# Attention running up to 1.9 batches ahead of the FFN, stores without one-row DMAs, and sparser filler matmuls

## The chip, the core and the metric
The kernel runs on one core of a Trainium2 chip. The metric is the device time of one execution in microseconds (us). The program is one launch; its instruction streams are fixed when it is built, one per engine: TensorE (PE), VectorE (DVE), ScalarE (ACT), GpSimd (POOL) and SyncE (SP). Engines wait for one another by semaphores only, and each works through its own stream in order.

## What is computed
Two stages, for 8 batches, 12 heads, 448 rows, head size 64 (model size 768), first layer of the FFN 3072 wide:

```
scores = (q @ k.T) / 8
x      = (relu(scores) ** 2 / 448) @ v          # heads side by side: 448 x 768 a batch
u      = x + real(fft(fft(x, axis=rows), axis=columns))
un     = (u - mean(u)) / sqrt(var(u) + 1e-6)    # over the 768 columns
out    = u + relu(un @ w_ch1) @ w_ch2
```

q, k, v, both weights and the output are float32 in HBM; matmuls are in bf16.

## The kernel before
**Attention** of a batch is 24 steps of two heads and one of four row chunks. A step is two scores matmuls into a psS buffer (L441), a relu on ACT into rsc (L473), a square on DVE into sq (L467), and two values matmuls into psT (L455). Four steps make one 128-column piece m of x, transposed (xT). DVE folds row s with row 448 - s into sums and differences (`fold`, L389 to L398), so that the Fourier transforms become real matmuls over 225 rows, and an SP DMA transposes xT back to rows (xn, L407). q and k are first copied (qkr, L339) and transposed, in batch 0 on TensorE, later by SP DMAs (qkT, L347). The loads of q, k, v and of the weights (w) are issued on POOL in one order; a q or k load waits for its buffer's copy, a v load for the values matmuls that read its buffer.

**Mix** of a batch: 24 matmuls (L618) with the column matrices `chan`, copies to pc (ACT L629, DVE L631), then in two chunks of rows, SC = 0 to 127 and 128 to 224, the row matmuls (L502), their evacuation (qs on ACT, tm and tp on DVE), the sums u for the upper rows (DVE) and mirrored lower rows (POOL; DVE in batch 0), the statistics (L535, L536), std on ACT (L539), and un on ACT (L549). u and un go to DRAM scratch: the upper rows by plain SP DMAs (utop, ntop), the lower ones, which come out in reverse order, by an indirect DMA on POOL (ubot, nbot, L569). The second chunk of the lower half has 97 rows, whose row 96 is row 0 of ubot and nbot: a one-row SP DMA writes it (L567), ahead of the indirect DMA of the other 96.

**FFN** works on groups of rows: 384 and 512 in turn, since group 2i takes the first 384 rows of batch 2i and group 2i+1 its last 64 with all of batch 2i+1. The transposed rows unT come from ntop and nbot by SP DMA transposes (`turn_un`, L592); only in group 0 TensorE transposes un (L651) and ACT copies it (L654). 24 blocks of six matmuls (L712) each with a relu into hT (L702) make the first layer; the second is 24 matmuls (L747) for each 128 rows and half of the columns, added to u (o, L729) and stored. psF has two buffers, psS and psT two each.

**The order** of all this is made when the program is built, by a planner (`Streams.run`): every part is a generator that announces its next piece of work with an engine, a cost in us, due times and buffers, and the planner always emits the piece that can start first by its own clock. Attention's pieces come last as long as `progress`, the FFN's share done in batches, is below `lead`:

```
lead = b + p / NP - LEAD
e = yield need("PE", dur + SWITCH, deps, bufs, lambda: progress[0] >= lead)
```

`warming` fills TensorE with 128x256 matmuls on zeros (L765) until the FFN begins. It too is planned: a filler is put wherever the planner believes TensorE to be idle, and on the chip it runs in its place, whether TensorE is idle then or not. `build_dft` makes the Fourier matrices from angles: products on DVE (L234, L243), reduction to one turn on DVE (L218, L220), sine on ACT (L222).

Of the kernel before, what the change touches and what calls it, by code (L numbers as in the profile page):

```python
# [9 lines left out]
FP32 = mybir.dt.float32  # L10
BF16 = mybir.dt.bfloat16
AF = mybir.ActivationFunctionType
ALU = mybir.AluOpType

# [28 lines left out]
class Streams:  # L43
    def __init__(self):
        self.engine = dict.fromkeys(LATENCY, 0.0)
        self.streams = []
        self.dma_free = 0.0
# [4 lines left out]
    def dma(self, start, nbytes, rate=350e3):  # L52
        self.dma_free = max(self.dma_free, start + 1.0) + nbytes / rate
        return self.dma_free + 1.2
# [60 lines left out]
def kernel(  # L115
# [9 lines left out]
    nc = tc.nc  # L125
# [12 lines left out]
    SC = [(0, 128), (128, NS)]  # L138
# [10 lines left out]
    ubot = [dram.tile([HS + 1, D], FP32, name=f"ubot{b}") for b in range(B)]  # L149
    ntop = [dram.tile([HS, D], BF16, name=f"ntop{b}") for b in range(B)]  # L150
    nbot = [dram.tile([HS + 1, D], BF16, name=f"nbot{b}") for b in range(B)]
# [17 lines left out]
    eps_t = const.tile([128, 1], FP32, name="eps_t")  # L169
    ident = const.tile([128, 128], BF16, name="ident")  # L170
# [11 lines left out]
    def dft_indices():  # L182
        nc.gpsimd.iota(drow[:, 0:2], pattern=[[128, 2]], base=0, channel_multiplier=1,
                       allow_small_or_imprecise_dtypes=True)
        nc.gpsimd.iota(drow[:, 4:7], pattern=[[128, 3]], base=0, channel_multiplier=1,
                       allow_small_or_imprecise_dtypes=True)
        nc.gpsimd.iota(dcol[:, 0:NS], pattern=[[1, NS]], base=0, channel_multiplier=0,
                       allow_small_or_imprecise_dtypes=True)
        nc.gpsimd.iota(dcol2, pattern=[[1, 2], [2, KH]], base=0, channel_multiplier=0,
                       allow_small_or_imprecise_dtypes=True)  # L190

    def small_constants():
        nc.vector.memset(zero_t, 0.0)
        nc.vector.memset(eps_t, 1e-6)
        nc.vector.memset(warm, 0.0)  # L195
# [13 lines left out]
    seq = const.tile([128, 2, 2, NS], BF16, name="seqm")  # L209
# [3 lines left out]
    def build_dft():  # L213
        def sincos(dst, y, n, p):

            e = yield need("DVE", n / 1920 + n / 960 + 0.3)
            r = work.tile([128, 4 * KH], FP32, name="dftr", tag="o", bufs=2)
            nc.vector.tensor_scalar(r[:p, :n], y[:p, :n], float(2 ** 23), float(2 ** 23),  # L218
                                    op0=ALU.add, op1=ALU.subtract)
            nc.vector.tensor_tensor(y[:p, :n], y[:p, :n], r[:p, :n], op=ALU.subtract)  # L220
            e = yield need("ACT", act(n), [e + LATENCY["DVE"]])
            nc.scalar.activation(dst, y[:p, :n], AF.Sin, bias=zero_t[:p], scale=2.0 * math.pi)  # L222
            dft_ready.t = e + LATENCY["ACT"]

        row, col, col2 = drow, dcol, dcol2
        e = yield need("DVE", 0.16, [indices_ready])
        nc.vector.tensor_scalar(row[:, 0:2], row[:, 0:2], 1.0 / S, None, op0=ALU.mult)
        nc.vector.tensor_scalar(row[:, 4:7], row[:, 4:7], 1.0 / D, None, op0=ALU.mult)

        for t in range(2):  # L230
            e = yield need("DVE", 0.5)
            y = work.tile([128, 4 * KH], FP32, name="dfty", tag="u", bufs=2)
            for i in range(2):
                nc.vector.tensor_scalar(y[:, i * NS:(i + 1) * NS], col[:, 0:NS],  # L234
                                        row[:, i:i + 1], 0.25 if t == 0 else 0.0,
                                        op0=ALU.mult, op1=ALU.add)
            yield from sincos(seq[:, t, :, :].rearrange("p a s -> p (a s)"), y, 2 * NS, 128)

        for m in range(3):
            e = yield need("DVE", 0.7)  # L240
            y = work.tile([128, 4 * KH], FP32, name="dfty", tag="u", bufs=2)
            for i in range(2):
                nc.vector.tensor_scalar(y[:, i * 2 * KH:(i + 1) * 2 * KH], col2,  # L243
                                        row[:, 4 + m:5 + m], 0.25 if i == 0 else 0.0,
                                        op0=ALU.mult, op1=ALU.add)
            yield from sincos(chan[m].rearrange("p a s -> p (a s)"), y, 4 * KH, 128)

        yield need("ACT", 1.5)
        nc.scalar.activation(row[:, 7:8], zero_t, AF.Sqrt, bias=eps_t)
# [7 lines left out]
    def load_group(i):  # L257
# [3 lines left out]
        for x, (nm, src) in enumerate((("q", q), ("k", k), ("v", v))):  # L261
# [6 lines left out]
            ready[i][x].t = sch.dma(e, GRP, 270e3)  # L268
# [17 lines left out]
    def load_w1(hf):  # L286
        for m in range(MC):
            e = yield need("POOL", 0.85)
            t = wpool.tile([128, FF // 2], BF16, name=f"w1_{m}_{hf}")
            nc.gpsimd.dma_start(  # L290
                out=t, in_=moe_w_ch1[m * 128:(m + 1) * 128, hf * (FF // 2):(hf + 1) * (FF // 2)])
            w1_sb[m][hf] = t
            done = sch.dma(e, 128 * FF * 2)
        w1_ready[hf].t = done

    def load_w2():
        for i in range(4):
# [5 lines left out]
            w2_ready[i].t = sch.dma(e, 768 * D * 4)  # L303
# [108 lines left out]
    def attention(b):  # L412
        G = 1 if b == 0 else 2
# [3 lines left out]
        for p in range(NP + 2):  # L417
# [6 lines left out]
            if p >= 2:  # L424
                ma, ca = divmod((p - 2) * G, 4)
                deps += [sqs[i][1] for i in range((p - 2) * G, (p - 1) * G)]
                if ca == 0:
                    bufs.append(BT)
                if p % (12 // G) == 2:
                    deps.append(ready[b * NG + ma // 2][2])  # L430
# [17 lines left out]
            if p >= 2:  # L448
# [45 lines left out]
    def mix_rows(b, ch, pcs):  # L494
# [5 lines left out]
        for t in range(2):  # L500
            for i, (n0, n1) in enumerate(SC):
# [55 lines left out]
    def store_rows(ch, top, bot, us, nbytes, t, cells):  # L557

        s0 = SC[ch][0]
# [9 lines left out]
        nc.gpsimd.indirect_dma_start(  # L569
            out=bot, out_offset=bass.IndirectOffsetOnAxis(ap=back[ch][:w], axis=0),  # L570
            in_=us[1][:w], in_offset=None)
        cells[2 * ch + 1].t = sch.dma(e, w * D * nbytes) + (1.5 if ch == 1 else 0.0)
# [34 lines left out]
    def mix(b):  # L607
# [3 lines left out]
        for n0, n1 in SC:  # L611
# [12 lines left out]
        for (n0, n1), (pp, t) in zip(SC, pps):  # L624
# [133 lines left out]
    def warming():  # L758
# [4 lines left out]
        while progress[0] == 0.0:  # L763
            e = yield need("PE", 0.12 if e > 5.0 else 0.23)
# [3 lines left out]
    LEAD = 1.6  # L768
# [42 lines left out]
```

## Time and profile before

| | |
|---|---|
| median of 3 runs | 719.48 us (717.96 to 722.58) |
| the profiled execution | 721.07 us, span 719.3 us |
| TensorE clock granted, mean | 0.955 |
| PE busy | 659.9 us (92%), 4109 matmuls, of them 517 fillers |
| DVE busy, ACT busy, POOL busy | 339.9, 327.8, 138.3 us |
| DMA | 85.57 MB, 169568 packets |

The span is the time from the first to the last instruction. Matmul ends are modelled and neighbours overlap, so a PE that is busy for 92% isn't at its peak for 92%: what a run of matmuls costs is read from start to start. "Idle before" in a row is the time for which that engine stood still just ahead of the instruction, and behind the arrow stands what ended it.

### The profile page before, as it was taken

To read this page: it belongs to the slowest core of one execution; us is meant where nothing else is said; L and a number is where in the kernel's file an instruction comes from. 1 tells how busy PE (TensorE), PEld (TensorE's weight loads), DVE (VectorE), ACT (ScalarE), POOL (GpSimd) and SP (SyncE) were. 2 spreads that over 40 slices of the span, in tenths; PEclk is the share of its full clock that TensorE was granted. 3 is DMA by queue.
4 is the path that set the end of the run, shared out by engine and by line. 5 is a ranking of instruction groups with operands and counts; after the bars stand their busy time and mean duration, and the time that the engine had idled before them with its cause. 6 is when DMAs were issued, how large, how long until landed. Compare 5 with 4: busy or idle time off the path is not lost.

```text
span 719.3 us, 10591 instructions
## 1 busy us (share of the span) xinstructions
PE 659.9 (92%) x4109; PEld 352.8 (49%) x4109; DVE 339.9 (47%) x779; ACT 327.8 (46%) x481; POOL 138.3 (19%) x173
## 2 busy tenths in 40 slices
PE   8999999885999899995999899994999899977997
PEld 6558844541446355651446355641446355643454
DVE  7577046682436544483336644483236744440011
ACT  3752287353643546453643546352553546222400
POOL 9223012231112301231112301221102300120000
PEclk9999999996999899996999999995999999998999
DMA  9999969959726687759526698549443632162012
GB/s 121 196 176 166 240 120 130 151 165 113 108 59 124 168 136 123 71 174 161 73 53 133 169 136 123 74 158 174 40 84 93 166 91 59 39 197 64 1 48 84
DMA packets 169568, 85.57 MB, mean 119 GB/s; under 512 B 152863, under 2 KB 157510, under 8 KB 169518
## 3 DMA queue, kind: packets, MB, share of 16 engines
q0 software_dynamic: 72528, 34.07, 36.7%
q1 hardware_dynamic: 96990, 50.83, 31.2%
q8 instruction: 32, 0.52, 0.3%
q14 instruction: 18, 0.15, 0.1%
HBM read 62.91 MB, written 27.07 MB: 125 GB/s over the span
## 4 chain that ended last, share of the span: by engine, by line
PE 81%; DVE 9%; DMA 5%; issue 2%; ACT 1%; SPq 1%; POOL 0%; DVEq 0%; POOLq 0%; ACTq 0%
PE psF L712 32%; PE psF L747 25%; PE psF L765 7%; PE psS L441 6%; PE psT L455 6%; DMA unT<-nbot 4%; PE psS L618 2%; DVE stats L535 2%; PE psS L502 1%; DVE u L524 1%; DVE sq L467 1%; ACT rsc L473 1%; DVE o L729 1%; DVE u L523 1%; DMA unT<-ntop 1%
## 5 line engine op out<-in xcount | busy, mean ns | idle before, releaser
L712 PE MATMUL psF<-unT,w 128*128 128x512 bf16 (+1 forms) x1152 | 233.7, 360 | 33.4 <-DMA unT<-nbot 24.6
L747 PE MATMUL psF<-w,hT 128*128 128x384 bf16 x1344 | 233.4, 331 | 0.0
L473 ACT ACTIVATE rsc<-psS 112x896 bf16<-112x896 f32 x192 | 170.5, 916 | 124.7 <-PE psS L441 93.2
L712 PEld LDWEIGHTS <-w 128*128 128x128 bf16 x1152 | 110.9, 99 | 153.3 <-issue 52.7
L747 PEld LDWEIGHTS <-hT 128*128 128x128 bf16 x1344 | 129.2, 99 | 100.0 <-issue 21.5
L467 DVE TENSOR_TENSOR sq<-rsc 112x896 bf16<-112x896 bf16 x192 | 114.8, 619 | 87.9 <-ACT rsc L473 87.6
L702 ACT ACTIVATE hT<-psF 128x384 bf16<-128x384 f32 (+1 forms) x192 | 104.7, 545 | 107.7 <-PE psF L712 107.6
L441 PE MATMUL psS<-qkT 64*112 64x448 bf16 x384 | 63.7, 381 | 17.3 <-ACT rsc L473 16.3
L729 DVE TENSOR_TENSOR o<-psF,o 128x384 f32<-128x384 f32 x56 | 30.5, 544 | 93.9 <-PE psF L747 91.9
L265 POOL DMA_DIRECT2D vn<-in_v_dram x24 | 20.4, 851 | 256.2 <-PE psT L455 254.0
L380 DVE TENSOR_SCALAR xT<-psT 128x224 bf16<-128x224 f32 x48 | 18.7, 391 | 101.5 <-PE psT L455 101.4
L765 PE MATMUL psF<-warm 128*128 128x256 bf16 x517 | 64.3, 279 | 1.1 <-DVE warm L195 1.1
L455 PE MATMUL psT<-sq,vn 112*64 112x448 bf16 x384 | 59.6, 381 | 0.0
L765 PEld LDWEIGHTS <-warm 128*128 128x128 bf16 x517 | 49.6, 100 | 12.2 <-issue 4.6
L441 PEld LDWEIGHTS <-qkT 64*112 64x112 bf16 x384 | 21.2, 125 | 54.6 <-issue 53.5
L549 ACT ACTIVATE un<-u,nmr,rstd 128x768 bf16<-128x768 f32 (+1 forms) x32 | 31.1, 1018 | 15.3 <-DVE nmr L544 15.3
L523 POOL TENSOR_TENSOR u<-tp,xn 128x385 f32<-128x385 f32 (+1 forms) x14 | 13.2, 945 | 128.6 <-DVE tp L513 110.9
L535 DVE BATCH_NORM_STATS2 stats<-u 128x6 f32<-128x384 f32 (+1 forms) x64 | 31.9, 539 | 0.0
L455 PEld LDWEIGHTS <-vn 112*64 112x64 bf16 x384 | 14.7, 109 | 32.5 <-issue 32.5
L569 POOL DMA_INDIRECT ubot<-u,back x16 | 18.2, 1137 | 57.5 <-DMA ubot<-u 49.3
L539 ACT ACTIVATE std<-mv,eps_t 128x2 f32<-128x2 f32 (+1 forms) x16 | 4.7, 296 | 50.3 <-DVE mv L536 50.3
L339 DVE COPY qkr<-kn 112x1024 bf16<-112x1024 bf16 x24 | 10.1, 422 | 32.0 <-DMA qkT<-qkr 32.0
(67 smaller groups left out, 358.1 us busy)
## 6 DMA issues: line engine op xcount, KB each, us to landing
out_dram<-o SPq DMA_DIRECT2D x28, 384.0 KB, 2.7
qn<-in_q_dram POOLq DMA_DIRECT2D x24, 224.0 KB, 6.6
kn<-in_k_dram POOLq DMA_DIRECT2D x24, 224.0 KB, 9.0
vn<-in_v_dram POOLq DMA_DIRECT2D x24, 224.0 KB, 5.4
w<-in_moe_w_ch_dram POOLq DMA_DIRECT2D x12, 384.0 KB, 15.3
w<-in_moe_w_ch_dram POOLq DMA_DIRECT2D x4, 1152.0 KB, 24.4
utop<-u SPq DMA_DIRECT2D x8, 384.0 KB, 6.1
o<-utop SPq DMA_DIRECT2D x8, 384.0 KB
```

The lines of the kernel that those rows point to most:

```text
L265: nc.gpsimd.dma_start(out=t, in_=src[b, hs].rearrange("h (f p j) d -> p (h f) (j d)", f=2, j=2))
L441: nc.tensor.matmul(sc[:R, h, 0:S].rearrange("k (c q) -> k c q", c=4), lhsT=kT[ps, m % 2, c, :], rhs=qT[ps, m % 2], start=True, stop=True)
L455: nc.tensor.matmul(av[h * Dh:(h + 1) * Dh, 0:S], lhsT=vn[:, c, h0 + h, :], rhs=sq[:, h, :], start=(c == 0), stop=(c == 3))
L467: nc.vector.tensor_tensor(sq, r, r, op=ALU.mult)
L473: nc.scalar.activation(r, sc[:R, :, 0:S], AF.Relu)
L535: nc.vector.bn_stats(stats[:n, hf, :], u[:n, hf * (D // 2):(hf + 1) * (D // 2)])
L549: nc.scalar.activation(un[:n], u[:n], AF.Identity, bias=nmr[:n, i:i + 1], scale=rstd[:n, i:i + 1])
L702: nc.scalar.activation(h[:, 0:N], ph[:, 0:N], AF.Relu)
L712: nc.tensor.matmul(ph[:, 0:N], lhsT=w1_sb[m][hf][:, jj * 128:(jj + 1) * 128], rhs=unT[:, m, 0:N], start=(m == 0), stop=(m == MC - 1))
L729: nc.vector.tensor_tensor(o[:, hs], pc[:, 0:D // 2], o[:, hs], op=ALU.add)
L747: nc.tensor.matmul(pc[:, 0:D // 2], lhsT=hT[j][:, c * 128:(c + 1) * 128], rhs=w2_sb[j // 6][:, j % 6, hs], start=(j == 0), stop=(j == JC - 1))
L765: nc.tensor.matmul(pw[:, 0:256], lhsT=warm[:, 0:128], rhs=warm, start=True, stop=True)
```

## The change
- `LEAD` goes from 1.6 to 1.9.
- The second chunk has 112 rows (128 to 239) wherever rows are mixed and stored; rows past 224 are surplus. `seq` and the column index get 240 columns. The scratch ubot and nbot grow to 384 rows, and the index of the second indirect store, `back[1]`, sends the 15 surplus rows into the part past the rows in use. The one-row DMAs go.
- Values follow scores by three steps instead of two in batch 0.
- Fillers past 6 us of the planner's clock are half a microsecond apart on that clock.
- The angles are made on ACT (a new constant, `quarter`, is the phase) instead of DVE.
- The planner keeps the DMAs of POOL and of SP in separate queues, and takes other rates for the weights.

```diff
-        self.dma_free = 0.0
+        self.dma_free = {"sw": 0.0, "hw": 0.0}
...
-    SC = [(0, 128), (128, NS)]
+    SC = [(0, 128), (128, 240)]
+    TC = [(0, 128), (128, NS)]
+    SX = 240
...
-    ubot = [dram.tile([HS + 1, D], FP32, name=f"ubot{b}") for b in range(B)]
+    UB = 384
+    ubot = [dram.tile([UB, D], FP32, name=f"ubot{b}") for b in range(B)]
...
-        for i in range(2):
-            nc.gpsimd.iota(back[i], pattern=[[0, 1]], base=HS - 128 * i, channel_multiplier=-1)
+        nc.gpsimd.iota(back[0], pattern=[[0, 1]], base=HS, channel_multiplier=-1)
+
+        v = const.tile([128, 2], FP32, name="backv")
+        nc.gpsimd.iota(v[:, 0:1], pattern=[[0, 1]], base=HS - 128, channel_multiplier=-1,
+                       allow_small_or_imprecise_dtypes=True)
+        nc.gpsimd.tensor_scalar(v[:, 1:2], v[:, 0:1], 0.0, float(UB), op0=ALU.is_lt, op1=ALU.mult)
+        nc.gpsimd.tensor_tensor(v[:, 0:1], v[:, 0:1], v[:, 1:2], op=ALU.add)
+        nc.gpsimd.tensor_copy(back[1], v[:, 0:1])
...
-                nc.vector.tensor_scalar(y[:, i * 2 * KH:(i + 1) * 2 * KH], col2,
-                                        row[:, 4 + m:5 + m], 0.25 if i == 0 else 0.0,
-                                        op0=ALU.mult, op1=ALU.add)
+                nc.scalar.activation(y[:, i * 2 * KH:(i + 1) * 2 * KH], col2, AF.Identity,
+                                     bias=quarter if i == 0 else zero_t, scale=row[:, 4 + m:5 + m])
...
-            done = sch.dma(e, 128 * FF * 2)
+            done = sch.dma(e, 128 * FF * 2, 380e3, "sw")
...
-        G = 1 if b == 0 else 2
+        G, LAG = (1, 3) if b == 0 else (2, 2)
...
-        if ch == 1:
-            e = yield need("SP", 0.1, [t[1]])
-            nc.sync.dma_start(out=bot[0:1, :], in_=us[1][w:w + 1])
         e = yield need("POOL", 1.1, [t[1]])
         nc.gpsimd.indirect_dma_start(
-            out=bot, out_offset=bass.IndirectOffsetOnAxis(ap=back[ch][:w], axis=0),
-            in_=us[1][:w], in_offset=None)
+            out=bot, out_offset=bass.IndirectOffsetOnAxis(ap=back[ch][:s1 - s0], axis=0),
+            in_=us[1][:s1 - s0], in_offset=None)
...
-            e = yield need("PE", 0.12 if e > 5.0 else 0.23)
+            e = yield need("PE", 0.12 if e > 5.0 else 0.23, [e + 0.5 if e > 6.0 else 0.0])
...
-    LEAD = 1.6
+    LEAD = 1.9
```

Line numbers shift by 7 to 10 (L712 becomes L719, L747 L754, L702 L709, L618 L625, L502 L512, L569 L576, L592 L599, L441 L451, L473 L483, L765 L772). Fillers fall from 517 to 118. Between the row matmuls of batch 0 and its transposes for group 0 stood 215 fillers; now 27, with eight scores matmuls of batch 1 among them.

The end of attention 0 on DVE before, from the copy of batch 1's k (its copy of q stands seven rows higher, among the squares) to the first copies of its last piece:

```order
L339 COPY qkr<-kn 112x1024
L396 TENSOR_TENSOR diff<-fold 128x450
L398 TENSOR_TENSOR fold<-fold 128x450
L467 TENSOR_TENSOR sq<-rsc 112x896 x3
L380 TENSOR_SCALAR xT_113<-psT 128x224
L383 TENSOR_SCALAR xT_113<-psT 128x224
```

and now:

```order
L349 COPY qkr<-qn 112x1024
L406 TENSOR_TENSOR diff<-fold 128x450
L408 TENSOR_TENSOR fold<-fold 128x450
L349 COPY qkr<-kn 112x1024
L477 TENSOR_TENSOR sq<-rsc 112x896 x2
L390 TENSOR_SCALAR xT_114<-psT 128x224
```

Both copies still stand ahead of the last squares and the last fold; the copy of q has come down behind the fold of piece 4. Further on, the copies of the next group, which stood behind the whole mix of batch 0, now stand inside it, between tp and u and between u and the statistics.

On ACT around the mix of batch 2, before (in the second layer of group 1; pc to un are the mix, rsc is attention 3, hT the FFN):

```order
L629 ACTIVATE pc<-psS 128x386
L629 ACTIVATE pc<-psS 97x386
L473 ACTIVATE rsc<-psS 112x896 x2
L508 ACTIVATE qs<-psS 128x385
L508 ACTIVATE qs<-psS 97x385
L539 ACTIVATE std<-mv,eps_t 128x2
L549 ACTIVATE un<-u,nmr,rstd 128x768 x2
L473 ACTIVATE rsc<-psS 112x896
L539 ACTIVATE std<-mv,eps_t 97x2
L473 ACTIVATE rsc<-psS 112x896
L549 ACTIVATE un<-u,nmr,rstd 97x768 x2
L473 ACTIVATE rsc<-psS 112x896 x10
```

and now, from qs on:

```order
L518 ACTIVATE qs<-psS 128x385
L709 ACTIVATE hT<-psF 128x512 x2
L518 ACTIVATE qs<-psS 112x385
L709 ACTIVATE hT<-psF 128x512 x2
L549 ACTIVATE std<-mv,eps_t 128x2
L709 ACTIVATE hT<-psF 128x512
L559 ACTIVATE un<-u,nmr,rstd 128x768 x2
L709 ACTIVATE hT<-psF 128x512 x2
L483 ACTIVATE rsc<-psS 112x896
L549 ACTIVATE std<-mv,eps_t 112x2
L483 ACTIVATE rsc<-psS 112x896
L559 ACTIVATE un<-u,nmr,rstd 112x768 x2
```

The mix has moved into the first layer of group 1, so hT of its last blocks stand between qs, std and un; the two relus of attention between the chunks are where they were. On TensorE the mix of batch 2 now stands behind block 14 of group 1's first layer (it stood behind the fourth of 32 pieces of its second layer), that of batch 1 behind block 23 of group 0, of batch 3 behind block 12 of group 2, and of batch 7 behind block 11 of group 6.

On POOL the four stores of a batch keep their places. SP's stream loses the one-row DMAs; before, for batch 1:

```order
L734 DMA out_dram<-o 128x768
L567 DMA ubot_78<-u 1x768
L563 DMA ntop_86<-un 128x768
L563 DMA ntop_86<-un 96x768
L567 DMA nbot_94<-un 1x768
L734 DMA out_dram<-o 128x768
```

and now:

```order
L573 DMA utop_70<-u 96x768
L573 DMA ntop_86<-un 128x768
L699 DMA o<-ubot_77 128x768
L741 DMA out_dram<-o 128x768
L573 DMA ntop_86<-un 96x768
L599 DMA_TRANSPOSE unT<-ntop_86 128x6x224
```

Nothing stands between the last store of un and the transposes any more.

More of the change, by code (lines that the diff above doesn't have):

```diff
@@ L46, in __init__, with dma @@
         self.streams = []
-        self.dma_free = 0.0
+        self.dma_free = {"sw": 0.0, "hw": 0.0}
     def add(self, gen, rank):
         self.streams.append([gen, rank, None])
-    def dma(self, start, nbytes, rate=350e3):
-        self.dma_free = max(self.dma_free, start + 1.0) + nbytes / rate
-        return self.dma_free + 1.2
+    def dma(self, start, nbytes, rate=350e3, queue="hw"):
+        self.dma_free[queue] = max(self.dma_free[queue], start + 1.0) + nbytes / rate
+        return self.dma_free[queue] + 1.2
     def run(self):
@@ L416, in attention @@
         av = None
-        for p in range(NP + 2):
+        for p in range(NP + LAG):
             m, c0 = divmod(p * G, 4)
@@ L500, in mix_rows @@
         for t in range(2):
-            for i, (n0, n1) in enumerate(SC):
+            for i, (n0, n1) in enumerate(TC):
                 nc.tensor.matmul(pq[:n, t, 0:KN], lhsT=seq[:n1 - n0, t, i, s0:s1],
@@ L610, in mix @@
         pcs, pps = [], []
-        for n0, n1 in SC:
+        for n0, n1 in TC:
             n = n1 - n0
@@ L623, in mix @@
             BA[m].free.append(e)
-        for (n0, n1), (pp, t) in zip(SC, pps):
+        for (n0, n1), (pp, t) in zip(TC, pps):
             n = n1 - n0
```

49 lines of the change are left out of this document (25 added, 24 removed).

## Prediction
> **What bounds the kernel now.** First the share of the chain that ended last, then that chain in order of time, where it leaves TensorE.
>
> ```profile
> PE 81%; DVE 9%; DMA 5%; issue 2%; ACT 1%; SPq 1%; POOL 0%; DVEq 0%; POOLq 0%; ACTq 0%
> ```
>
> Four fifths of the end time is TensorE. So I first work out what its work costs when nothing interrupts it, from long pieces of the chain (start us, us, what) and from the counts of the groups of instructions:
>
> ```profile
> 87.84 0.98 PE psF L712 x6
> 280.68 0.52 PE psS L441 x4
> 281.19 0.50 PE psT L455 x4
> 281.69 4.01 PE psF L712 x24
> 301.10 1.32 PE psS L502 x8
> 344.48 5.29 PE psF L712 x24
> 618.91 2.00 PE psS L618 x24
> 684.05 31.21 PE psF L747 x192
> ```
>
> ```profile
> L747 PE MATMUL psF<-w,hT 128*128 128x384 bf16 x1344 | 233.4, 331 | 0.0
> L712 PE MATMUL psF<-unT,w 128*128 128x512 bf16 x576 | 134.9, 394 | 33.3 <-DMA unT<-nbot 24.6 <-issue 8.7
> L712 PE MATMUL psF<-unT,w 128*128 128x384 bf16 x576 | 98.8, 326 | 0.1
> L441 PE MATMUL psS<-qkT 64*112 64x448 bf16 x384 | 63.7, 381 | 17.3 <-ACT rsc L473 16.3 <-DVE pc L631 0.9
> ```
>
> The first FFN block starts at 87.84. Behind it stand 576 wide first-layer matmuls at 5.29/24 = 0.220 us, 576 narrow ones at 0.167, 1344 second-layer ones at 31.21/192 = 0.163, for seven batches 336 scores and as many values matmuls at 0.13 and 0.125 (four in 0.52 and 0.50), seven mixes of 2.00 and seven row mixes of 1.32: 127 + 96 + 219 + 86 + 14 + 9 = 551 us. The last matmul ends at 684.05 + 31.21 = 715.3, and 4.0 us of last add and store follow to the span of 719.3. 87.8 + 551 + 4 = 643 against 719.3: **76 us** after the first FFN block are lost on TensorE. Where the chain leaves it longest:
>
> ```profile
> 134.63 2.01 PE psS L618 x24
> 163.87 8.93 DMA unT<-nbot
> 172.85 4.50 PE psF L712 x12
> 295.33 2.00 PE psS L618 x24
> 327.64 8.37 DMA unT<-nbot
> 336.06 7.41 PE psF L712 x24
> 490.32 9.59 DMA unT<-nbot
> 500.04 7.33 PE psF L712 x24
> 645.98 5.42 issue
> 651.41 32.65 PE psF L712 x144
> ```
>
> FFN groups 1, 3, 5 and 7 each wait for the transpose that brings in their last rows, which hangs on the mix (L618) of the newest batch. The four cost 8.9 + 8.4 + 9.6 us, and 8.7 for the last (the idle time under "issue" in the L712 row), and then the matmuls run slower at first: 24 take 7.41 where 5.29 is usual, twelve 4.50 where 2.65 is, and the last 144 lose 32.65 - 31.7 = 0.9. Together 42.5 us. 33 us remain: 16.3 is TensorE waiting before scores for ACT's relu (L441 row above), the rest is small change at switches between kinds of matmul and slow starts after these waits.
>
> **The first 87.8 us** are bound differently.
>
> ```profile
> 47.36 0.43 DVE L339 COPY qkr<-qn 112x1024 bf16<-112x1024 bf16 x1 [0.41 <-DMA qn<-in_q_dram]
> 49.43 0.43 DVE L339 COPY qkr<-kn 112x1024 bf16<-112x1024 bf16 x1
> 56.13 0.40 DVE L398 TENSOR_TENSOR fold<-fold 128x450 bf16<-128x450 bf16 x1
> 61.40 23.47 PE psF L765 x215
> 73.49 1.95 ACT L549 ACTIVATE un<-u,nmr,rstd 97x768 bf16<-97x768 f32 x2 [0.43 <-DVE nmr L544]
> 85.27 2.23 ACT L654 ACTIVATE unT<-psS 128x768 bf16<-128x768 f32 x3 [9.83 <-PE psS L651]
> ```
>
> ```profile
> 20.00:40.00 20.00, 19.90 (x153) 10.87 (x151) 12.29 (x28) 14.82 (x20) 6.46 (x10) 1.00 1.08 200
> ```
>
> The normalized rows of batch 0 are there at 73.49 + 1.95 = 75.4, but TensorE first works off 215 fillers that stand ahead of its transposes, to 84.9: 9.4 us given away. And q of batch 1 lands only at 47.3: the DMA engines are full with the loads ahead of it (the share of 1.08 in the last but one column of the window, behind TensorE's clock of 1.00).
>
> **The change part by part. Start.** Attention 0 gets faster by itself (values a step later, filler clusters of 8 to 20 cut to 0 to 5, the angle arithmetic of the Fourier matrices moved from DVE to the idle ACT). Little of that counts: DVE now has the copies of batch 1's q and k ahead of the last two squares and the last fold. q lands at 47.3 and k no later than 49.4, so the last fold can't end, and the mix start, before about 49.9 + 1.1 (two squares) + 0.7 (values) + 2.0 (fold) = 53.7, where it was 56.13 + 0.40 = 56.5: -3 us. From there to the finished rows it took 75.4 - 56.5 = 18.9; now two more copies (0.7), a square and a relu (1.4) stand in that stretch. Behind the rows now only 8 fillers stand. Then 2.9 us of transposes and copies as before (84.9 to 87.8) plus about 2 us (a relu ahead of the copies, and four scores and four values matmuls ahead of FFN 0). With TensorE at full rate FFN 0 would start near 53.7 + 18.9 + 2.1 + 4.9 = 79.6.
>
> But TensorE now idles through most of this, and the rows after the four waits show that it then runs at half rate for its next 3 to 4 us (7.41 for 24 against 5.29; twelve in 4.50 against 2.65). I charge the mix, the row mix and the transposes with 3 us and FFN 0's first blocks with 2. The Trainium skill, page "TensorE: Matmul & The Clock Gate", Part 1, says this of a window of about 3.4 us: an idle window halves the clock, a busy one restores it. It speaks against the sparse fillers; by it the start pays these 5 us, and with a clock that stays up it pays none. The four waits bear the rule out; no row shows sparse fillers, so I keep 0 and 8 us as bounds. Start of FFN 0: 84.6 in effect, against 87.8. In return 16 matmuls of batch 1 (2 us) are then done. Net **-5 us**, between -12 (a clock that stays up, and copies and relus hidden) and +5 (8 us of half rate, and loads that land 7 us later).
>
> **One-row DMAs.** The last batch shows their price, since nothing else is in its way:
>
> ```profile
> 636.64 1.94 ACT L549 ACTIVATE un<-u,nmr,rstd 97x768 bf16<-97x768 f32 x2 [0.43 <-DVE nmr L544]
> 637.93 0.91 POOL L569 DMA_INDIRECT ubot<-u,back  x1 [5.33 <-DMA ubot<-u]
> 639.15 1.00 POOL L569 DMA_INDIRECT nbot<-un,back  x1 [0.30 <-issue]
> 643.83 0.91 POOL L569 DMA_INDIRECT nbot<-un,back  x1 [3.68 <-DMA nbot<-un]
> 647.44 1.25 SPq L592 DMA_TRANSPOSE unT<-nbot  x1
> ```
>
> The second store of u waits 5.33 us on POOL for the one row's landing, both stores of the normalized rows queue behind it, and the second of those again waits 3.68. The last rows are ready at 638.6; without the one-row DMAs their store can go at once instead of at 643.83: the chain from mix to transposed rows gets **5.2 us** shorter, in every batch. 112 rows in place of 96 or 97 cost nothing that I can price: the 97-row and 128-row forms of a group took the same (296 and 295 ns in the std rows below).
>
> **Lead 1.9.** The mix of batch b moves from early in the second layer of group b-1 into its first layer (for batch 1, to the end of group 0's first layer). What the chain needs is read from mix start to first wide matmul: 172.85 - 134.63 = 38.2 for batch 1, 336.06 - 295.33 = 40.7 for batch 3, 651.41 - 618.91 = 32.5 for batch 7; less 5.2: 33, 35.5 and 27.3. What TensorE has to do meanwhile, by the new order and the rates above: batch 1, the mix, 144 second-layer matmuls, the row mix, 44 of attention: 2 + 23.5 + 1.3 + 5.6 = 32.4, so some **1 to 2 us of waiting stay** at group 1. Batch 3: the mix, 66 + 144 matmuls, the row mix, 76 of attention: 2 + 11 + 23.5 + 1.3 + 9.7 = 47.5, over 35.5. Batch 7: 2 + 12 + 1.3 + 23.5 = 38.8, over 27.3. So three of four waits go with their slow starts, and most of the first: **-41 us**.
>
> What is late next? In the old order ACT had nothing queued behind the statistics of the mix; now the first layer's relus (hT) are, and TensorE can run only two blocks ahead of them (psF has two buffers, 2 x 6 x 0.22 = 2.6 us wide, 2.0 narrow).
>
> ```profile
> L539 ACT ACTIVATE std<-mv,eps_t 97x2 f32<-97x2 f32 x8 | 2.4, 296 | 16.8 <-DVE mv L536 16.8
> L539 ACT ACTIVATE std<-mv,eps_t 128x2 f32<-128x2 f32 x8 | 2.4, 295 | 33.5 <-DVE mv L536 33.5
> ```
>
> Per batch ACT waits 33.5/8 = 4.2 us before the first std and 2.1 before the second. In the new order two hT stand between qs and std, so some of it is filled. I take 2 us of new TensorE waits a batch (bounds 0 and 6.3, the whole of both): **+14 us**. Of the old 16.3 us before scores I expect 5 to stay, since the runs of scores and values without an FFN block between them (just ahead of each of the waits) shrink from three steps to one, and the mix no longer lies between them: **-11 us**. The extra load of ACT tables in the new order stands where ACT waits for DVE's angles, at nothing.
>
> **The sum.** 719.3 - 5 - 41 + 14 - 11 = 676; slow starts after the old waits before scores (3 places, some 2 us each) go too: -6. Span **670 us**. The profiled run took 721.07, 1.8 over its span, and 1.6 over the median of 719.48, so the median should stand where the span does: 670.
>
> **Rivals.** (a) The relus wait for almost nothing, 0 to 0.5 us a batch (-12 on 670), and the start gains its 12 in place of 5: 670 - 12 - 7 = 651. For it: the two hT between qs and std stand just where ACT waited before. (b) The transposes stay the bound: SP's queue and the DMA of eight transposes a batch hold the chain to 40 us and more also without the one-row DMAs. Then batch 1 waits 8 and batch 7 2, and the slow starts come back, 670 + 12 = 682; with the start at its +5, 692. For it: unT<-nbot took 8 to 10 us to land three times. Against: batch 3's cover is 12 us longer than its chain. (c) Slower than before: hT behind std and un on ACT. If every wait of ACT in the mix stops TensorE, and DVE, which also has copies that wait for transposes in there, is later still, each of seven batches loses that much. It decides at 2 + 49/7 = 9 us a batch; the sum of both std waits is 6.3, which would give 670 + 30 = 700. At 10 us it gives 726. Only DVE waits of 4 us more on top of every chain reach it.
>
> **How the numbers follow.** Forecast (657 to 680) 0.52; (a) 0.2; (b) 0.16; (c) near 700 0.05, beyond 712 0.07. Range 647 to 695: it leaves out the end of (a) and of (c). A measurement of this kernel tells about 1%, 7.2 us: faster 0.93, same 0.04, slower 0.03.
>
> **What would show it.** Right: no wait of L712's successor for unT<-nbot over 2 us but at group 1; FFN 0 starting between 77 and 86, on copies done right behind a landing at 47; POOL without waits for a one-row landing; L712 after the start at half rate for some us. Wrong: q of batch 1 landing later than 50 (the start then slips with it); waits of TensorE's first layer for hT of more than 3 us a batch, with ACT in std or un; scores ahead of the batch 0 transposes waiting for their transposed q and k.

## The result and the profile after

| | before | changed |
|---|---|---|
| median of 4 runs | 719.08 us (717.96 to 722.58) | 662.17 us (661.54 to 664.21) |
| ratio, 95% interval | | 0.9206, 0.9168 to 0.9243 |
| profiled execution, span | 721.07, 719.3 us | 661.54, 659.8 us |

The kernel is faster by 57 us. The forecast was 670, in a range of 647 to 695. The share of the chain that ended last, on the changed kernel's page:

```profile
PE 78%; DMA 8%; DVE 6%; ACT 4%; issue 2%; SPq 1%; POOL 0%; DVEq 0%; POOLq 0%; ACTq 0%
```

TensorE leads as before, but DMA has more of it (8% where it had 5%). First the part from the first FFN block on, as one window of each kernel (start and end in us, length, then busy us and count of PE, PEld, DVE, ACT, POOL; then granted clock, DMA share, GB/s), before and after:

```profile
88.00:715.00 627.00, 575.17 (x3393) 290.53 (x3390) 287.11 (x653) 287.85 (x430) 106.26 (x111) 0.95 0.60 111
```

```profile
91.00:656.00 565.00, 556.01 (x3377) 284.46 (x3377) 285.94 (x651) 279.54 (x426) 103.36 (x109) 1.00 0.67 124
```

Sixteen matmuls fewer, since they are done ahead of this window, and otherwise the same work, in 62 us less and with a clock of 1.00 where it was 0.95. TensorE's longest wait in this window is 2.3 us; before, it stood still for 6.9 to 9.6 us at each of the four stops. The groups of instructions of TensorE and of ACT's std (busy us, mean ns, then idle time before them and what ended it) correspond to those shown of before:

```profile
L719 PE MATMUL psF<-unT,w 128*128 128x512 bf16 x576 | 130.1, 379 | 0.1
L719 PE MATMUL psF<-unT,w 128*128 128x384 bf16 x576 | 100.5, 326 | 0.7 <-ACT hT L709 0.6
L754 PE MATMUL psF<-w,hT 128*128 128x384 bf16 x1344 | 227.7, 326 | 0.5 <-ACT hT L709 0.5
L451 PE MATMUL psS<-qkT 64*112 64x448 bf16 x384 | 67.3, 409 | 20.4 <-DMA qkT<-qkr 9.6 <-ACT rsc L483 7.7 <-DVE tp L523 3.1
L549 ACT ACTIVATE std<-mv,eps_t 128x2 f32<-128x2 f32 x8 | 2.3, 289 | 14.0 <-DVE mv L546 14.0
L549 ACT ACTIVATE std<-mv,eps_t 112x2 f32<-112x2 f32 x8 | 2.4, 298 | 5.8 <-DVE mv L546 5.7
```

The wide first layer waits for 0.1 us in all (33.3 before): the four waits for unT<-nbot are gone. The relus hT hold TensorE up for 0.6 + 0.5 us in the whole kernel. The chain in order of time, at groups 1 and 7:

```profile
129.18 2.00 PE psS L625 x24
...
162.55 8.16 DMA qkT<-qkr
170.75 0.58 PE psS L451 x4
172.67 0.60 ACT hT L709
...
593.51 31.08 PE psF L719 x144
624.59 31.21 PE psF L754 x192
```

What TensorE waits for near group 1 is now q and k of batch 2, not unT. The last group runs through from 593.51 to 655.80. By the rates of the prediction the work from the first FFN block at 90.92 on is 548.5 us (16 matmuls were done before it), so TensorE loses 655.8 - 90.9 - 548.5 = **16 us** behind it where it lost 76.

The start went the other way. DVE's timeline, from the last fold of attention 0 through the mix of batch 0, the second chunk's un on ACT, and the first FFN block (start, us, engine, line, and in brackets the idle time before it):

```profile
60.84 0.40 DVE L408 TENSOR_TENSOR fold<-fold 128x450 bf16<-128x450 bf16 x1
...
66.77 0.42 DVE L349 COPY qkr<-qn 112x1024 bf16<-112x1024 bf16 x1
...
68.51 0.55 DVE L534 TENSOR_TENSOR u<-tp,xn 128x383 f32<-128x383 f32 x1
74.80 0.43 DVE L349 COPY qkr<-kn 112x1024 bf16<-112x1024 bf16 x1 [5.74 <-DMA qkT<-qkr]
75.14 1.02 DVE L545 BATCH_NORM_STATS2 stats<-u 128x6 f32<-128x384 f32 x2
```

```profile
84.25 1.93 ACT L559 ACTIVATE un<-u,nmr,rstd 112x768 bf16<-112x768 f32 x2
```

```profile
90.92 1.15 PE L719 MATMUL psF<-unT,w 128*128 128x384 bf16 x6
```

The last fold, for which the mix waits, ends at 61.2, where it was 56.5. The copy of the next group's k stands between u and the statistics; its buffer is free only when the DMA transpose of the k before has landed, and DVE stands still for 5.74 us. The normalized rows are ready at 86.2, where it was 75.4, and the first block starts 3.2 us later than before (87.68 in this view), without the 215 fillers.

### The profile page after: what moved, and what is told of

Read it like the earlier page. It is cut to its first block, busy times and chain, and to the rows that moved or that the text cites. A ratio compares the mean times of both kernels' runs of the same rounds, so it can differ in the third digit from the quotient of the medians.

```text
span 659.8 us, 9754 instructions
## 1 busy us (share of the span) xinstructions
PE 622.0 (94%) x3710; PEld 315.3 (48%) x3710; DVE 336.8 (51%) x770; ACT 329.6 (50%) x492; POOL 136.2 (21%) x176
## 4 chain that ended last, share of the span: by engine, by line
PE 78%; DMA 8%; DVE 6%; ACT 4%; issue 2%; SPq 1%; POOL 0%; DVEq 0%; POOLq 0%; ACTq 0%
PE psF L754 33%; PE psF L719 27%; PE psT L465 7%; PE psS L451 7%; DMA qkT<-qkr 6%; DMA o<-utop 2%; PE psS L625 2%; ACT rsc L483 1%; PE psF L772 1%; PE psS L512 1%; DVE stats L545 1%; ACT dfty L254 1%; DVE u L534 1%; DVE dfty L232 0%; ACT un L559 0%
## 5 line engine op out<-in xcount | busy, mean ns | idle before, releaser
L483 ACT ACTIVATE rsc<-psS 112x896 bf16<-112x896 f32 x192 | 169.5, 915 | 141.0 <-PE psS L451 94.5
L719 PE MATMUL psF<-unT,w 128*128 128x512 bf16 (+1 forms) x1152 | 230.6, 353 | 0.8 <-ACT hT L709 0.6
L754 PE MATMUL psF<-w,hT 128*128 128x384 bf16 x1344 | 227.7, 326 | 0.5 <-ACT hT L709 0.5
L754 PEld LDWEIGHTS <-hT 128*128 128x128 bf16 x1344 | 127.8, 98 | 98.4 <-issue 17.1
L719 PEld LDWEIGHTS <-w 128*128 128x128 bf16 x1152 | 108.6, 98 | 113.7 <-issue 19.5
L709 ACT ACTIVATE hT<-psF 128x384 bf16<-128x384 f32 (+1 forms) x192 | 104.2, 544 | 93.1 <-PE psF L719 92.7
L451 PE MATMUL psS<-qkT 64*112 64x448 bf16 x384 | 67.3, 409 | 20.4 <-DMA qkT<-qkr 9.6
L465 PE MATMUL psT<-sq,vn 112*64 112x448 bf16 x384 | 61.5, 390 | 0.6 <-DVE sq L477 0.6
L451 PEld LDWEIGHTS <-qkT 64*112 64x112 bf16 x384 | 21.5, 131 | 58.6 <-issue 44.6
L772 PE MATMUL psF<-warm 128*128 128x256 bf16 x118 | 28.5, 375 | 1.1 <-DVE warm L201 1.1
L349 DVE COPY qkr<-kn 112x1024 bf16<-112x1024 bf16 x24 | 12.1, 505 | 25.7 <-DMA qkT<-qkr 25.7
L576 POOL DMA_INDIRECT nbot<-un,back x15 | 15.0, 1001 | 39.9 <-ACT un L559 22.8
L275 POOL DMA_DIRECT2D qn<-in_q_dram x24 | 20.3, 847 | 13.5 <-DVE diff L406 7.0
L275 POOL DMA_DIRECT2D kn<-in_k_dram x24 | 20.8, 868 | 7.9 <-DVE qkr L349 5.5
```

The lines of the kernel that those rows point to most:

```text
L275: nc.gpsimd.dma_start(out=t, in_=src[b, hs].rearrange("h (f p j) d -> p (h f) (j d)", f=2, j=2))
L451: nc.tensor.matmul(sc[:R, h, 0:S].rearrange("k (c q) -> k c q", c=4), lhsT=kT[ps, m % 2, c, :], rhs=qT[ps, m % 2], start=True, stop=True)
L465: nc.tensor.matmul(av[h * Dh:(h + 1) * Dh, 0:S], lhsT=vn[:, c, h0 + h, :], rhs=sq[:, h, :], start=(c == 0), stop=(c == 3))
L483: nc.scalar.activation(r, sc[:R, :, 0:S], AF.Relu)
L709: nc.scalar.activation(h[:, 0:N], ph[:, 0:N], AF.Relu)
L719: nc.tensor.matmul(ph[:, 0:N], lhsT=w1_sb[m][hf][:, jj * 128:(jj + 1) * 128], rhs=unT[:, m, 0:N], start=(m == 0), stop=(m == MC - 1))
```

## The experiments
All twelve in one table. The mix columns are the starts of the mixes of batches 1 and 2 on TensorE, read from its timeline; "first block" is the start of the FFN. The kernel before had a median of 719 to 721 us in each session, so kernels of different sessions are compared by their ratio to it. At half clock the mix of batch 0 starts with two matmuls that then wait for the last fold, so the end of that fold is given where it counts.

| run | median us | ratio (95%) | first block | mix 1 | mix 2 |
|---|---|---|---|---|---|
| changed kernel | 662.2 | 0.921 (0.917 to 0.924) | 90.9 | 129.0 | 190.8 |
| lead 1.6 | 695.7 | 0.964 (0.957 to 0.971) | 91.4 | 133.1 | 209.6 |
| one-row DMAs back | 670.7 | 0.929 (0.925 to 0.932) | 91.6 | 129.7 | 197.2 |
| before, lead 1.9 | 673.9 | 0.932 (0.929 to 0.936) | 87.7 | 134.5 | 206.5 |
| dense fillers | 670.5 | 0.929 (0.925 to 0.932) | 99.8 | 135.6 | 197.4 |
| batch 1 kept behind | 668.3 | 0.927 (0.923 to 0.930) | 83.8 | 135.4 | 198.3 |
| the same, dense | 668.2 | 0.926 (0.922 to 0.929) | 80.1 | 133.2 | 198.5 |
| the same, 0.25 us apart | 667.2 | 0.923 (0.918 to 0.928) | 85.7 | 139.0 | 202.2 |
| the same, no fillers | 660.4 | 0.919 (0.914 to 0.923) | 78.2 | 125.4 | 188.1 |
| late weights | 666.8 | 0.928 (0.924 to 0.932) | 86.7 | 132.1 | 191.0 |
| no fillers | 659.4 | 0.917 (0.913 to 0.920) | 87.0 | 125.6 | 188.8 |
| late weights, no fillers | 663.1 | 0.923 (0.920 to 0.926) | 81.6 | 126.7 | 184.8 |
| another start | 663.2 | 0.920 (0.917 to 0.923) | 79.7 | 129.0 | 194.2 |

### What the lead did
```diff
-    LEAD = 1.9
+    LEAD = 1.6
```


> The changed kernel with LEAD back at 1.6, all else kept. Theory (the lead removes the four stops, and with them the waits before scores): the stops return, each shorter by the 5.2 us of the one-row DMAs, 42.5 - 21 = 21 us, and most of the 16 us before scores: 662 + 21 + 13 = 696, with waits of 3 to 5 us for unT<-nbot at groups 1, 3, 5 and 7. Rival (the shorter chain alone removes the stops, the lead is only more cover): under 675, no wait for unT<-nbot over 1 us.

695.65 us. The first theory held. TensorE's waits (us in total, times, longest):

```profile
PE psS L451 <- ACT rsc L483: 22.2, 22, 2.9
PE psF L719 <- DMA unT<-nbot: 9.8, 2, 5.6
```

The waits before scores are back, 14.5 us more than the 7.7 of the changed kernel. Of the four stops two show, 4.2 and 5.6 us at groups 5 and 7, each with a slow start; at group 3 the first 24 matmuls take 6.9 us where 5.3 is usual, and group 1 starts without a loss. The time came out as worked out, its parts only roughly.

The other side of it, the kernel before with nothing but the lead:

```diff
-    LEAD = 1.6
+    LEAD = 1.9
```


> The kernel before with LEAD 1.9 and nothing else. Theory (the lead does nearly all): the body loses its stops but for 5 to 7 us at group 1, the start keeps its dense fillers and its 87.7 us to the first FFN block: 664 to 670, so that all other parts of the change together are worth 2 to 8 us. Rival (the parts other than the lead carry a third or more of the 57 us): over 681.

673.9 us, 4 us above the range of the first theory and 7 below the rival. The lead alone is worth 47 of the 57 us. The parts overlap, though: with lead 1.6 kept, all the others together gain 26 us (695.7 against 721.3 in that session), since they shorten the same stops. What is left over is at group 1:

```profile
PE psF L712 <- DMA unT<-nbot: 8.7, 1, 8.7
PE psS L441 <- ACT rsc L473: 5.0, 10, 0.8
```

One wait of 8.7 us for unT, and no other: with lead 1.9 the chain of each later mix is covered even with the one-row DMAs in it.

### What the one-row DMAs cost
```diff
+        if ch == 1:
+            e = yield need("SP", 0.1, [t[1]])
+            nc.sync.dma_start(out=bot[0:1, :], in_=us[1][w:w + 1])
...
-            out=bot, out_offset=bass.IndirectOffsetOnAxis(ap=back[ch][:s1 - s0], axis=0),
-            in_=us[1][:s1 - s0], in_offset=None)
+            out=bot, out_offset=bass.IndirectOffsetOnAxis(ap=back[ch][:w], axis=0),
+            in_=us[1][:w], in_offset=None)
```


> The changed kernel with the one-row DMAs put back ahead of the second indirect stores (96 rows in the indirect store), lead 1.9 kept. Theory (the chain is 5.2 us longer, and with lead 1.9 only group 1 has too little cover): group 1 waits 3 to 5 us for unT<-nbot and starts slowly, the other groups wait for nothing: 666 to 669. Rival 1 (with lead 1.9 the one-row DMAs are hidden everywhere): 662. Rival 2 (the chains of all groups are bare): 680 and more.

670.7 us, 6 us more by the ratios and 8.6 by the medians. The size is near the first theory's, the place is not:

```profile
PE psS L451 <- DMA qkT<-qkr: 10.0, 2, 6.1
...
PE psF L757 <- DVE o L739: 2.8, 1, 2.8
...
PE psF L722 <- DMA unT<-nbot: 1.2, 1, 1.2
```

Only 1.2 us are waits for unT, and 2.8 are one for the old rows that the FFN adds to. The wait of 6.1 us is ahead of the first FFN block, where the changed kernel has one of 7.3. The other 4.0 us are at group 1, for the transposed q and k of batch 2 (2.3 in the changed kernel), and TensorE restarts slowly there:

```profile
166.32 8.03 DMA qkT<-qkr
174.39 0.99 PE psS L451 x4
175.39 0.89 PE psT L465 x4
176.28 4.84 PE psF L722 x12
182.13 2.69 PE psF L722 x12
```

The transpose takes as long as in the changed kernel (8.03 us, 8.16 there), but starts 3.8 us later. It goes through SP's queue, as the one-row DMAs do; what delays its start was not tried.

The chains themselves can be read from the traces. From the start of a mix to the start of the last transpose of its rows (unT<-nbot on SP), in us:

| | batch 1 | batch 3 | batch 5 | batch 7 |
|---|---|---|---|---|
| before: one-row DMAs, lead 1.6 | 29.4 | 32.5 | 33.9 | 28.7 |
| without them, lead 1.6 | 27.4 | 28.0 | 28.6 | 25.7 |
| one-row DMAs back, lead 1.9 | 29.9 | 28.5 | 28.8 | 25.9 |
| changed kernel: without them, lead 1.9 | 26.3 | 27.8 | 27.8 | 25.9 |

With lead 1.9 they cost the chain 3.6 us at batch 1 and 0 to 1.0 at the others. The last store of the normalized rows does start 2.8 to 3.4 us later with them in each of the four batches, but the transpose behind it mostly doesn't. With lead 1.6 the difference is 2.0 to 5.3 us, with the rest of the change in it.

### The start: fillers or waits
```diff
-            e = yield need("PE", 0.12 if e > 5.0 else 0.23, [e + 0.5 if e > 6.0 else 0.0])
+            e = yield need("PE", 0.12 if e > 5.0 else 0.23, [0.0])
```


> The changed kernel with dense fillers again (none of the half microsecond between them), all else kept. Theory (sparse fillers drop TensorE to half its clock from 10 to 56 us and from 70 to 92 us, which costs more than the fillers did): clock 1.0 from 10 us on, the scores of attention 0 in 0.33 us a pair in place of 0.55, the mix of batch 0 starts near 56 in place of 59.5, and the first FFN block at 85 to 88 in place of 90.9: 656 to 659. Rival 1 (the start hangs on the copy of k and the transposed q and k of batch 1, not on TensorE's clock): first block at 90 to 92, 661 to 663. Rival 2 (dense fillers stand in the way again): 665 and more.

670.5 us: rival 2 in its number, but not in its reason. The clock was 1.0 from 20 to 60 us, and the mix of batch 0 started at 58.1, 1.4 us earlier (its last fold ended at 58.0, 3.2 us earlier). Then DVE stopped twice in that mix:

```profile
72.30 0.43 DVE L349 COPY qkr<-kn 112x1024 bf16<-112x1024 bf16 x1 [10.49 <-DMA qkT<-qkr]
...
90.54 0.43 DVE L349 COPY qkr<-kn 112x1024 bf16<-112x1024 bf16 x1 [6.92 <-DMA qkT<-qkr]
```

The planner had put a second pair of copies into the mix, and the first block came at 99.8. To separate the two, the next four keep batch 1 (beyond its first copy) behind the first FFN block. But for the fillers, the order on TensorE, ACT and POOL is then the same in the first three; the first copies of batch 1 on DVE move by a few places in one of them, and in the fourth, without fillers, also some pieces of attention 0 and of the first FFN group:

```diff
+                                   lambda: progress[0] > 0.0 or b == 0 or (b == 1 and g == 0))
...
-            e = yield need("PE", dur + SWITCH, deps, bufs, lambda: progress[0] >= lead)
+            e = yield need("PE", dur + SWITCH, deps, bufs,
+                           lambda: progress[0] >= lead and (b == 0 or progress[0] > 0.0))
```


> The changed kernel, fillers as they are (0.5 us apart), but nothing of batch 1 beyond its first copy of q and k is put ahead of the first FFN block: DVE's copies of the later groups stand behind the whole mix of batch 0, the twelve scores and four values matmuls of batch 1 behind the first FFN block. Theory (the copies that wait for transposed q and k inside the mix hold up the start): the normalized rows of batch 0 are ready near 80 in place of 86, the first FFN block at 83 to 86 in place of 90.9, less 2 us of matmuls that are then still to do: 655 to 659. Rival (TensorE at half its clock holds up the start, the copies only fill the time): first block at 89 to 91, 662 to 664.

```profile
83.75 2.13 PE L721 MATMUL psF<-unT,w 128*128 128x384 bf16 x6
```

The first block came as the theory has it, and the kernel took 668 us, not 657. So an earlier start of the FFN need not bring an earlier end. Attention 1 stands wholly behind it now, a pair of steps for two FFN blocks in TensorE's order, and its mix starts 6 us later (135.4): it also stands behind 48 matmuls of the second layer (7.8 us) that stood behind it in the changed kernel. The edit moves more than the waits, then, and this run alone doesn't tell the two apart; the last run below starts the FFN early in the changed kernel's order. On the chain there stands, once more, a transpose of q or k:

```profile
80.66 16.38 DMA qkT<-qkr
97.50 0.63 DVE sq L479
98.21 0.49 ACT rsc L485
99.03 0.49 ACT hT L711
```

From the mix of batch 2 on these runs do the same: TensorE's last matmul ends 465 us after its start, in the changed kernel (190.8 to 655.8) as in the dense run (197.4 to 662.3) and in this one (198.3 to 663.3). What counts in the start is when the mix of batch 2 can begin, 62 to 65 us behind that of batch 1 in the runs that change only fillers or keep batch 1 behind.

With the same order and dense fillers:

> As the run with the copies and scores of batch 1 kept behind, but with dense fillers, 132 of them between the row matmuls of batch 0 and its transposes. Theory (with those waits gone, a full clock pays): mix of batch 0 at 58, normalized rows at 77, the fillers done at 77, first FFN block at 80: 651 to 655, 3 to 5 us under the run with sparse fillers. Rival (TensorE's clock counts for nothing here, since loads and DVE set the pace): within 1 us of the run with sparse fillers, or above it.

668.2 us, the rival's. The first block is 3.7 us earlier (80.1), and TensorE then stands still for 5.0 us between two blocks of the first group, where it had stood for 2.8. The mix of batch 1 starts 2.2 us earlier, that of batch 2 no earlier: dense fillers with their full clock bought nothing at the end.

With fillers 0.25 us apart on the planner's clock:

> As the run with the copies and scores of batch 1 kept behind, with fillers 0.25 us apart. It asks what TensorE's clock follows. Theory 1 (it follows the full-width matmuls, 128 rows by 128 columns, of which the fillers are the only ones in attention 0; the scores and values matmuls use 64 rows or 64 columns): twice the fillers bring the clock back to 1.0 somewhere between 20 and 50 us. Theory 2 (it follows how much of the time TensorE is busy at all): TensorE was already back to back at half clock with sparse fillers without getting it back, so it stays at 0.5 until 56. Time 652 to 658, nearer to the dense run by theory 1, to the sparse run by theory 2.

It told nothing on the clock: in the stretch in question, 30 to 50 us, TensorE did 87 matmuls, against 86 with 0.5 us, so the fillers were not doubled there. Its four times spread from 660.9 to 672.9 and the profile is of the longest, so nothing is concluded from its row in the table.

With none:

> As the run with the copies and scores of batch 1 kept behind, with no fillers at all past 6 us of the planner's clock. TensorE at half clock until well into the first FFN group. If fillers at half clock only take time from attention 0 (a step took 0.55 + 0.52 + 0.33 us, of which 0.33 is the filler): mix of batch 0 at 55 to 57 in place of 59.5. Then mix, row mix and transposes at half clock: first FFN block at 81 to 85, and its first 3 to 4 us at half rate: 654 to 660. Rival (loads set attention 0's pace): mix no earlier than 58, 658 to 663.

660.4 us, the quickest of the four. Attention 0 gets shorter by 5.7 us by the start of the mix (54.1) and by 4.9 by its last fold, at half clock all the while: the rival, that loads set its pace, falls. The later loads wait for buffers that attention 0 frees, so they move up as well (the last of w2 lands at 88 in place of 95), and batch 1 with them (125.4).

### The start: what the transposes wait for
DVE's wait in the mix is a DMA transpose that took 13.6 us to land. The four loads of w2 (4.7 MB) were issued beside it.

```diff
-            e = yield need("POOL", 1.1)
+            e = yield need("POOL", 1.1, ok=lambda: un_ready[0][1].t is not None)
```


> The changed kernel with the four loads of the second layer's weights issued behind the first stores of batch 0's mix instead of ahead of it; every other instruction keeps its place. Theory (DVE's copy of k inside the mix waits for a DMA transpose that shares the DMA engines with those 4.7 MB): the transposes of q and k of batch 1 land within 7 us of their issue, in place of 14 to 18; DVE does not wait between u and the statistics; first FFN block at 83 to 86 in place of 90.9, the mix of batch 1 at 122 to 125 in place of 129.0, 655 to 658. Rival 1 (the transposes are slow by themselves): 661 to 663. Rival 2 (the weights come late for the second layer, which starts at 131): TensorE waits there for them, 664 and more.

666.8 us. The first half held: DVE no longer waits between u and the statistics, its waits for these transposes fall (the first line is of the changed kernel, the other two are of this run), and the first block starts at 86.7. So the transposes are not slow by themselves.

```profile
DVE qkr L349 <- DMA qkT<-qkr: 28.4, 14, 7.7
```

```profile
DVE qkr L349 <- DMA qkT<-qkr: 14.6, 12, 2.5
DVE qkr L349 <- DMA qn<-in_q_dram: 8.2, 1, 8.2
```

Then the weights collide with the next pairs: TensorE waits 7.5 us, up to 112.0, for a transpose that was issued at 93.8, and the load of the q behind it comes late, too. The mix of batch 1 is later than in the changed kernel, not earlier. Behind it the planner has made another order, with the mix of batch 2 behind 11 blocks of group 1's first layer instead of 15 (block 14, counted from 0), so 470 us follow its start in place of 465; the starts of mix 2 of the two runs with late weights can't be compared with the others. Without fillers, and with both:

> The changed kernel with no fillers past 6 us of the planner's clock, all else in its place. Theory (at half clock the fillers only take time from attention 0): the mix of batch 0 at 54 in place of 59.5, the wait of DVE's copy of k stays (its transposes are slow for the weights' loads): first FFN block at 86 to 89, mix of batch 1 at 125 to 127, 657 to 660. Rival (the wait takes up all that attention 0 gains): 661 to 663.

> The late weights and no fillers together. If the two holds (the transposes behind the weights, the fillers at half clock) are independent and both real: first FFN block at 78 to 81, mix of batch 1 at 117 to 120, 650 to 653, under the changed kernel by 9 to 12 us. If only one of them counts, the time is that of the better of the two single runs.

659.4 and 663.1 us. No fillers: mix of batch 0 at 54.1 and first block at 87.0 as expected, and 3 us better by the median, with an interval that overlaps the changed kernel's. The two together are no sum: the late weights cost what they bring here, too. The last run split the weights two and two and put the angles back on DVE:

```diff
-            e = yield need("POOL", 1.1)
+            e = yield need("POOL", 1.1, ok=lambda: i < 2 or un_ready[0][1].t is not None)
...
-            e = yield need("ACT", 1.1)
+            e = yield need("DVE", 0.7)
...
-        while progress[0] == 0.0:
+        while e < 6.0:
```


> A try at a better start: the changed kernel with no fillers past 6 us of the planner's clock, the angles of the Fourier matrices back on DVE, and the four loads of the second layer's weights two and two (two where they were, two behind the first stores of batch 0's mix). TensorE's order is that of the run without fillers. If a start is bound by the loads and by what DMA transposes wait behind them: first scores at 12 to 13 us, mix of batch 0 at 52 to 53, transposes of q and k of batch 1 landing within 10 us of their issue both before and after the first FFN block, that block at 77 to 81, mix of batch 1 at 118 to 122, 650 to 655. Rival (each hold that goes uncovers the next, as in the runs with the late weights): first block earlier, TensorE waiting for transposed q and k in the first FFN group, 657 to 662.

```profile
79.68 3.29 PE L721 MATMUL psF<-unT,w 128*128 128x384 bf16 x12
...
107.52 2.08 PE L721 MATMUL psF<-unT,w 128*128 128x384 bf16 x6 [10.16 <-ACT hT L711]
```

663.2 us, 1 us above the rival's range and in the rival's way: mix of batch 0 at 51.7, the first block 11 us earlier (in the changed kernel's order on TensorE, but for fillers and a step of attention 0), and 11 us lost in the first group (hT stands on ACT behind a relu, and that behind squares and a copy on DVE that waits for its load). It also shows what the angles cost. The end of attention 0 without fillers, with the angles on ACT and then on DVE:

```profile
55.95 0.40 DVE L408 TENSOR_TENSOR fold<-fold 128x450 bf16<-128x450 bf16 x1
```

```profile
53.57 0.40 DVE L410 TENSOR_TENSOR fold<-fold 128x450 bf16<-128x450 bf16 x1
```

The move to ACT made attention 0 longer by 2.4 us: ACT loads its table of functions twice there, 1.28 us each at 4.4 and 8.2, in the line of the angles. No run beats the changed kernel beyond its interval.

## Why the prediction was right, and where not
The sign and the place of the gain were right: the four stops were by far the largest term. The forecast was 8 us too high, mostly through two terms that missed in opposite directions.

- **The four stops, -41 us: right.** All four are gone. The transposed rows of batch 3 landed 35.1 us after the start of the mix (worked out as 35.5), of batch 7 29.2 (27.3); that of batch 1 30.7 (33), so that even the 1 to 2 us kept at group 1 didn't come. Lead 1.6 loses some 32 us again, lead 1.9 alone gives 47 of the 57. That the lengths came so close is in part luck, since each had been shortened by 5.2 us for the one-row DMAs (below). The stops had also been sized by three landings on the chain (8.9, 8.4 and 9.6 us); TensorE itself waited 24.6 us for these three by its row, 2.3 less, so that -39 would have been due.
- **Waits before scores, -11 us: right.** From 95 us on TensorE waits 5.1 us for rsc; 5 were to stay. **Slow starts, -6: right**, by the clock of 1.00 in the window.
- **hT behind std and un, +14 us: wrong.** It cost 1.1 us. The step that failed is that 2 us of ACT's waits a batch become TensorE's. Of the 19.8 us that ACT now waits before std, 10.1 are in batch 0's first chunk, before the FFN has begun, and 0.6 in its second; the other seven batches have 9.1, or 1.3 us each in place of 6.3. The two hT between qs and std fill the rest, as rival (a) said. Its time, 651, was not reached because of the start.
- **The start, -5 us net: wrong.** It became +3.2 us, less 2.1 for the sixteen matmuls done: +1. With TensorE at full rate the first block was to start at 79.6; it started 11.3 us later, of which 5 were charged to the half rate. 7.5 of the 11.3 came ahead of the mix: the last fold ended at 61.2, where 53.7 had been worked out from the landing of q alone. Attention 0 didn't get faster by itself. At half clock with its fillers it took 4.9 us longer than without them, and the move of the angles to ACT, with the extra table load put at nothing, cost another 2.4; without both, the last fold ended at 54.0. The other 3.9 came between there and the normalized rows, where I had priced the copies of the next group at their busy time, 0.7 us. The copy of k waited 5.74 us for the transpose ahead of it, with the statistics and the second chunk behind it on DVE. Rows of before showed the cause (the window at a DMA share of 1.08), but I had charged the full DMA engines to the loads alone. The text named the sign of it, scores ahead of the transposes that wait for q and k, and put no price on it.
- **TensorE's clock:** the half rate came, and far longer than the 5 us charged.

```profile
30.00:50.00 20.00, 20.00 (x86) 6.84 (x85) 12.57 (x31) 12.06 (x16) 4.09 (x5) 0.50 1.31 182
```

The clock is 0.50 with TensorE busy by the profile for all of the 20 us (a step is scores, values and a filler, 0.55 + 0.52 + 0.33 us, over and over; ends of matmuls are modelled, starts are not). By the Trainium skill, page "TensorE: Matmul & The Clock Gate", Part 1, one busy window of some 3.4 us restores the clock; here 20 us that the profile counts as busy did not, and the measurement decides. What the clock follows is open. At the end it did not matter: dense fillers with a clock of 1.00 gave the same time in the same order.
- **One-row DMAs, 5.2 us a chain in every batch: mis-sized.** With lead 1.9 they cost 3.6 us at batch 1, 0.7 and 1.0 at batches 3 and 5, and nothing at batch 7, on which the 5.2 was read. I had taken all of the later store for a later transpose, but in the changed kernel's batch 7 the store starts 3.4 us earlier and the transpose no earlier. Only group 1 has much use for it. **Rival (b)** fell with the first wait, **rival (c)** with hT.

So the sum was 13 us too high for ACT and 6 too low for the start: 663, and the span is 659.8.

## What to carry to other kernels
Give a chain of stores and transposes a cover that is longer than it, worked out from its own length; 0.3 batches of lead alone gave four fifths of this gain, and with them the shorter chain mattered only where the cover still fell short. Ask of a moved instruction not what it takes but what it waits for, and what stands behind it on its engine. Before an early stage is made shorter, look for what the second batch waits for: here the FFN could start 11 us earlier without a gain, since the next q and k then came late, beside the loads of the weights, and each hold that was taken away uncovered the next.

## What the hardware showed
How long a DMA transpose of q or k takes, in the changed kernel from 200 to 640 us, and twice on its chain beside the weights' loads:

```profile
DMA to landing us min/median/max: 2.6/3.0/8.0
```

```profile
61.12 13.59 DMA qkT<-qkr
...
75.29 17.63 DMA qkT<-qkr
```

3.0 us in the middle of the kernel, and 13.6 and 17.6 with 4.7 MB of loads ahead of it or beside it. With these loads moved behind it, DVE didn't wait for it any more. Fillers that are meant to keep TensorE's clock up can cost more than the clock: attention 0 was quicker at 0.50 without any (last fold done at 56.4) than at 1.00 with dense ones (58.0).
